# Pooled attention and a Gelu MLP on one core: the order of the first loads, w_in's halves, q's transposes of batch 1 and the last store

## The chip, the cores and the metric

The kernel runs on one core of a Trainium2 chip. The core has TensorE (PE), VectorE (DVE), ScalarE (ACT), GpSimd (POOL) and SyncE (SP), and 16 DMA engines which the queues of SP, ACT and POOL share. The metric is the device time of one execution in microseconds; lower is better.

## What is computed

```python
# q, k, v: (8 batches, 8 heads, 576 positions, 64) float32
k_p = k.reshape(B, H, Sp, 8, D).mean(axis=3)        # Sp = 72: means of 8 neighbours
v_p = v.reshape(B, H, Sp, 8, D).mean(axis=3)
attn = softmax(q @ k_p.T / sqrt(D))
x = (attn @ v_p) laid out as (4608 tokens, 512)
h = x @ w_in                                        # w_in: (512, 2048)
g = gelu_tanh(h)
out = g @ w_out                                     # w_out: (2048, 512), out: (4608, 512) float32
```

The matmuls run in bf16 with float32 sums.

## The kernel before

**Tiling.** Attention goes by batch, 8 of them with 576 columns each; its result is written transposed into `xT` (512 features as KO = 4 blocks of 128 partitions, 4608 columns). The MLP goes by groups of 512 columns (NG = 9). In each group phase 1 (`p1_mm`, L396) makes 16 tiles `fo` of h, each from 4 matmuls over `ko`, and `gelu` (L402) writes them to `gT`; phase 2 (`p2_mm`, L405) makes 4 row tiles of 128 rows of the output, 16 matmuls each, which `store` (L408) copies out of PSUM and sends off as 4 DMAs of 32 rows. The attention of batch g + 1 is woven into group g: pooling and transposes hang on tiles of phase 1 through `side` and `plan`, and scores, exponentials and products on matmul numbers of phase 2 through `todo`. The order on every engine is the order of the program text.

**The loads.** k and v come in as float32, q and the weights are turned to bf16 by the DMA. Before any computing the queues are given, in this order: k of batch 0 and a rest of v on SP and ACT (`load_k`, L74 to L77), v of batch 0 on SP and ACT (`load_v`, L90: 64 partitions each), and on GpSimd's queue q of batch 0 in two halves (L95), the identity matrix, w_in in two halves (L114), k of batch 1 (L74, L75, L77), q of batch 1 (L95) and w_out in four quarters (L121). w_in's halves are halves of its 2048 columns, each with all 4 blocks of rows: `w_in_b[0]` serves `fo` 0 to 7 and `w_in_b[1]` serves 8 to 15. v of batch 1 is issued on SP once VectorE has written one element of its tile (L485).

**Batch 0.** It is computed by itself ahead of group 0. VectorE pools k (L150), TensorE transposes k (L212) and q (L236), then come scores (L267), exponentials on ScalarE (L274), sums of exponentials (L349), logarithms and reciprocals (L354, L356), and VectorE's pooling of v (`v_steps`, L150 on `vt`, into `vz`), the products (L363) and the scaling into `xT` (L367). `spin` (L421) is a matmul of zeros that keeps TensorE busy. Group 0's first eight matmuls take `fo` 0 to 3 with `ko` 0 and 1, the next eight the same with `ko` 2 and 3.

**Batch 1, in group 0.** `plan` puts k's pooling at tile 0, `v_moves` (L183, a small DMA issued by ScalarE) at tile 7, the four transposes of q (`QG`) at tiles 12 to 15, with those of k at 13, and the pooling of half of v at 15. Attention starts in phase 2 at matmul number 6.

**The end.** The last row tile of the last group is made as two pieces of 384 and 128 columns (L617 to L626). Each is copied by VectorE and sent off as 4 DMAs of 32 partitions, two on ACT and two on SP:

```python
for n in range(4):
    b, col = divmod(N - 128 + n * 32, S)
    rows = out[b * S:(b + 1) * S].rearrange("(p t e) d -> e t p d", t=TP, e=2)
    (nc.sync if n % 2 else nc.scalar).dma_start(
        out=rows[col // CH, col % CH // 32][:, c0:c1], in_=osb[n * 32:(n + 1) * 32])
```

The 128 columns of `gT` that make a row tile stand as 4 blocks of 32, and rows that are neighbours within a block lie 18 output rows apart.

The softmax here doesn't subtract the row's maximum and nothing guards it: scores larger than these inputs give would overflow.

## Time and profile before

| what | us |
|---|---|
| median of 3 runs | 302.13 (302.08 to 303.34) |
| profiled execution | 303.02 |
| its span | 301.2 |
| TensorE busy, of the span | 292.1 |
| q, first half of batch 0: issue to landing | 8.2 |
| w_in, two halves: issue to landing | 14.6 and 19.4 |
| k of batch 1: issue to landing | 22.4 |
| last matmul ends | 297.4 |

The profile is one execution, taken by the hardware profiler. Its span is counted from the first instruction; all times below are from there. A line of the timeline gives start, length, engine, line, operation and tiles, and in brackets the idle time before it and what ended that. DMA issues have a line of their own with a q at the engine's name (SPq, ACTq); their length is that of issuing, not of the transfer. In the chain of waits each piece released the next.

### The profile page before, as it was taken

How to read it: one execution, taken by the hardware profiler on the slowest of the kernel's cores; microseconds unless marked ns; L12 is line 12 of the kernel's file. 1: busy time of each engine (PE TensorE's matmuls, PEld its weight loads, DVE VectorE, ACT ScalarE, POOL GpSimd, SP SyncE). 2: the span in 40 equal slices, each digit the busy share in tenths (PEclk: the TensorE clock that was granted, in tenths of full speed). 3: DMA queues.
4: the chain of work that ended last, by engine and by line, in shares of the span. 5: the costliest groups of instructions: out<-in, count | busy, mean ns of one | idle time of the engine just before them, and what ended most of it. 6: DMA issues, size and time to landing. Idle time of an engine off the chain costs nothing.

```text
span 301.2 us, 4348 instructions
## 1 busy us (share of the span) xinstructions
PE 292.1 (97%) x1498; PEld 151.4 (50%) x1527; DVE 149.6 (50%) x299; ACT 216.6 (72%) x408; POOL 37.6 (12%) x67
## 2 busy tenths in 40 slices
PE   8899999999999999999999999999999999999994
PEld 3465555554555455545554555455545555445443
DVE  3775577484577256815690659155924630110012
ACT  1596589879978898789877988798879887206500
POOL 7104001300600060005000410032000000000000
PEclk9999999999999999999999999999999999999998
DMA  7999986970798269935994399729961310121022
GB/s 223 263 242 268 252 175 127 255 185 12 169 265 174 48 153 248 187 72 120 247 202 89 90 254 208 106 51 252 236 119 36 74 37 0 37 70 36 0 72 70
DMA packets 39366, 43.11 MB, mean 143 GB/s; under 512 B 25584, under 2 KB 26224, under 8 KB 39216
## 3 DMA queue, kind: packets, MB, share of 16 engines
q0 software_dynamic: 8512, 24.39, 35.7%
q1 hardware_dynamic: 30080, 17.13, 25.0%
q10 hardware_dynamic: 752, 1.32, 1.3%
q8 instruction: 12, 0.20, 0.3%
q14 instruction: 10, 0.08, 0.1%
HBM read 36.70 MB, written 9.44 MB: 153 GB/s over the span
## 4 chain that ended last, share of the span: by engine, by line
PE 87%; DMA 7%; POOL 1%; DVE 1%; issue 1%; ACTq 0%; ACT 0%; DVEq 0%; POOLq 0%
PE PS L405 41%; PE PS L396 38%; DMA kt<-in_v_dram 7%; PE PS L322 4%; PE PS L311 2%; DVE kt L150 1%; PE PS L296 1%; PE PS L287 1%; PE PS L267 1%; POOL w_in_b L114 0%; POOL qb L95 0%; PE PS L236 0%; ACTq L183 0%; ACT gT L402 0%; POOL kt L74 0%
## 5 line engine op out<-in xcount | busy, mean ns | idle before, releaser
L405 PE MATMUL PS<-w_out_b,gT 128*128 128x512 bf16 (+2 forms) x575 | 138.0, 373 | 0.9 <-issue 0.2
L396 PE MATMUL PS<-xT,w_in_b 128*128 128x512 bf16 x565 | 125.9, 379 | 1.0 <-ACT gT L402 0.4
L402 ACT ACTIVATE gT<-PS 128x512 bf16<-128x512 f32 x144 | 79.2, 606 | 46.2 <-PE PS L396 46.2
L396 PEld LDWEIGHTS <-w_in_b 128*128 128x128 bf16 x576 | 65.0, 113 | 59.1 <-issue 0.7
L405 PEld LDWEIGHTS <-gT 128*128 128x128 bf16 x592 | 56.5, 97 | 52.5 <-issue 1.7
L340 DVE TENSOR_TENSOR xT<-PS,rc 64x288 bf16<-64x288 f32 x112 | 51.0, 455 | 20.5 <-ACT rc L332 17.8
L410 DVE COPY osb<-PS 128x512 f32<-128x512 f32 x35 | 24.2, 691 | 64.7 <-PE PS L405 61.4
L317 ACT ACTIVATE eT<-PS 64x576 bf16<-64x576 f32 x48 | 30.7, 640 | 0.6
L304 DVE COPY eT<-er 8x576 bf16<-8x576 bf16 x24 | 7.3, 302 | 39.9 <-ACT er L302 39.4
L329 ACT ACTIVATE ld<-PS 64x288 f32<-64x288 f32 x56 | 22.5, 402 | 5.6 <-PE PS L322 5.1
L332 ACT ACTIVATE rc<-ld 128x288 f32<-128x288 f32 x56 | 24.8, 443 | 1.8
L373 ACT ACT_TABLE_LOAD x17 | 21.8, 1283 | 3.6 <-issue 3.3
L150 DVE TENSOR_TENSOR kt<-kt 128x1280 f32<-128x1280 f32 (+5 forms) x18 | 18.9, 1048 | 10.0 <-DMA kt<-in_v_dram 6.0
L330 ACT ACTIVATE ld<-PS 64x288 f32<-64x288 f32 x56 | 22.5, 402 | 1.4
L322 PE MATMUL PS<-eT,vp 72*128 72x288 bf16 x96 | 19.7, 285 | 0.1
L150 DVE TENSOR_TENSOR vt<-vt 128x1024 f32<-128x1024 f32 (+3 forms) x18 | 17.1, 952 | 1.1 <-DMA vt<-in_v_dram 0.8
L502 POOL COPY gate<-eT 1x2 bf16<-1x2 bf16 x5 | 0.9, 177 | 125.6 <-DMA eT<-er 125.6
L322 PEld LDWEIGHTS <-vp 72*128 72x128 bf16 x96 | 9.5, 98 | 11.3
L421 PE MATMUL PS<-idle 128*128 128x512 bf16 x32 | 10.4, 466 | 1.6 <-DVE idle L139 1.2
L274 ACT ACTIVATE e<-PS 72x576 bf16<-72x576 f32 x16 | 9.9, 644 | 2.6 <-PE PS L267 2.4
L311 PE MATMUL PS<-qT,kx 128*128 128x288 bf16 x48 | 9.8, 286 | 0.0
L82 POOL DMA_DIRECT2D kt<-in_k_dram x12 | 7.5, 630 | 2.1 <-issue 2.1
(61 smaller groups left out, 115.0 us busy)
## 6 DMA issues: line engine op xcount, KB each, us to landing
out_dram<-osb SPq DMA_DIRECT2D x140, 64.0 KB
kt<-in_k_dram POOLq DMA_DIRECT2D x12, 512.0 KB, 6.5
vt<-in_v_dram POOLq DMA_DIRECT2D x12, 512.0 KB, 10.2
qb<-in_q_dram POOLq DMA_DIRECT2D x7, 576.0 KB, 14.7
w_in_b<-in_moe_w_in_dram POOLq DMA_DIRECT2D x2, 1024.0 KB, 17.0
w_out_b<-in_moe_w_out_dram POOLq DMA_DIRECT2D x4, 512.0 KB, 24.1
vt<-in_v_dram SPq DMA_DIRECT2D x3, 512.0 KB
kt<-in_k_dram POOLq DMA_DIRECT2D x1, 1024.0 KB, 22.4
```

What stands on the lines that cost most here:

```text
L150: nc.vector.tensor_tensor(out=o, in0=a, in1=b, op=ALU.add)
L317: nc.scalar.activation(out=eT[0:64, 2 * pr:2 * pr + 2, c, :], in_=PS[64 * c:64 * c + 64, 2:4, :CH], func=ACT.Exp, scale=1.0 / 64.0)
L322: nc.tensor.matmul(out=PS[:, bank + x, :CH], lhsT=window(vps[b % 2], 2 * pr + x), rhs=eT[:, 2 * pr + x, c, :], start=True, stop=True)
L329: nc.scalar.activation(out=ld[0:64], in_=PS[64:128, bank, :CH], func=ACT.Ln)
L330: nc.scalar.activation(out=ld[64:128], in_=PS[0:64, bank + 1, :CH], func=ACT.Ln)
L332: nc.scalar.activation(out=rc, in_=ld, func=ACT.Exp, scale=-1.0)
L340: nc.vector.tensor_tensor(out=xT[rows, pr, col:col + CH], in0=PS[rows, bank + x, :CH], in1=rc[rows], op=ALU.mult)
L373: nc.scalar.preload_act_table_set(name)
L396: nc.tensor.matmul(out=PS[:, h_bank(g, fo), :], lhsT=w, rhs=xT[:, ko, r0:r0 + GROUP], start=(ko == 0), stop=(ko == KO - 1))
L402: nc.scalar.activation(out=gTs[g][:, fo, :], in_=PS[:, h_bank(g, fo), :], func=ACT.Gelu_apprx_tanh)
L405: nc.tensor.matmul(out=PS[:, bank, c0:c1], lhsT=gTs[g][:, fo, r * 128:(r + 1) * 128], rhs=w_out_b[:, fo, c0:c1], start=(fo == 0), stop=(fo ...
L410: nc.vector.tensor_copy(out=osb, in_=PS[:, bank])
```

## The change

Four edits.

- **The loads.** `load_v(0)` stands behind `load_k(1)`, after a new GpSimd memset of one element of its tile, so that SP and ACT issue it when GpSimd has come that far in its own queue.
- **w_in.** The halves are halves of its rows: `w_in_b[0]` holds `ko` 0 and 1 for all 2048 columns, `w_in_b[1]` holds `ko` 2 and 3. `p1_mm` picks its operand accordingly.
- **q of batch 1.** Three of its four transposes and k's move one tile later in `plan`; the fourth goes into phase 2 at matmul number 2.
- **The last row tile.** VectorE copies its 128 columns of `gT`, four tiles at a time, into the idle `kts` tiles in another order (position in the block outermost, block innermost). The matmuls of the last row tile take these copies, so that the rows come out in an order in which 4 neighbouring partitions belong to 4 rows of `out` at a fixed distance, and each piece is one DMA of 128 partitions: ACT's for the 384 columns, SP's for the 128.

```diff
-    w_in_b = [consts.tile([128, KO, 1024], BF16, name=f"w_in_b{i}") for i in range(2)]
+    w_in_b = [consts.tile([128, KO // 2, DF], BF16, name=f"w_in_b{i}") for i in range(2)]
...
     load_k(0, [nc.sync, nc.scalar])
-    load_v(0, [nc.sync, nc.scalar])
     load_q(0, 0, 1)
     load_q(0, 1, 2)
     make_identity(nc, identb)
 
     def load_w_in(i):
-        nc.gpsimd.dma_start(out=w_in_b[i], in_=w_in_v[:, :, i * 1024:(i + 1) * 1024])
+        nc.gpsimd.dma_start(out=w_in_b[i], in_=w_in_v[:, 2 * i:2 * i + 2])
 
     load_w_in(0)
     load_w_in(1)
     load_k(1, [nc.gpsimd])
+
+    nc.gpsimd.memset(vts[0][:, 0, 0:1], 0.0)
+    load_v(0, [nc.sync, nc.scalar])
     load_q(1)
...
-        q, j = divmod(fo % 8, 4)
-        w = w_in_b[fo // 8][:, ko, q * 512 + j:(q + 1) * 512:4]
+        q, j = divmod(fo, 4)
+        w = w_in_b[ko // 2][:, ko % 2, q * 512 + j:(q + 1) * 512:4]
...
-                plan = {0: kk[:-1], 7: kk[-1:], 12: tq[:1], 13: tq[1:2] + tk, 14: tq[2:3], 15: tq[3:] + [lambda: v_half(1, 0)]}
+                plan = {0: kk[:-1], 7: kk[-1:], 13: tq[:1], 14: tq[1:2] + tk, 15: tq[2:3] + [lambda: v_half(1, 0)]}
...
+        if g + 1 == NG:
+
+            gLs = [kts[i // 2].rearrange("p r c -> p (r c)").bitcast(BF16)[:, i % 2 * 512:i % 2 * 512 + 512]
+                   .rearrange("p (f c) -> p f c", f=4) for i in range(4)]
+            for i, o in enumerate(gLs):
+                side[4 * i + 3].append(lambda i=i, o=o: nc.vector.tensor_copy(
+                    out=o.rearrange("p f (x t) -> p f t x", t=4),
+                    in_=gTs[g][:, 4 * i:4 * i + 4, 384:].rearrange("p f (t x) -> p f t x", t=4)))
...
             if g == 0:
+                at(2, trans_q, nb, *QG[3], 5, nc.vector)
                 at(18, v_half, 1, 1)
...
-            p2_mm(g, 3, fo, bank, c0, c1)
+            nc.tensor.matmul(out=PS[:, bank, c0:c1], lhsT=gLs[fo // 4][:, fo % 4], rhs=w_out_b[:, fo, c0:c1],
+                             start=(fo == 0), stop=(fo == FO - 1))
         osb = opool.tile([128, c1 - c0], F32, name="osb")
         nc.vector.tensor_copy(out=osb, in_=PS[:, bank, c0:c1])
-        for n in range(4):
-            b, col = divmod(N - 128 + n * 32, S)
-            rows = out[b * S:(b + 1) * S].rearrange("(p t e) d -> e t p d", t=TP, e=2)
-            (nc.sync if n % 2 else nc.scalar).dma_start(
-                out=rows[col // CH, col % CH // 32][:, c0:c1], in_=osb[n * 32:(n + 1) * 32])
+        b, col = divmod(N - 128, S)
+        t = col % CH // 32
+        rows = out[b * S:(b + 1) * S].rearrange("(p t e) d -> e p t d", t=TP, e=2)
+        (nc.sync if c0 else nc.scalar).dma_start(out=rows[col // CH, :, t:t + 4, c0:c1], in_=osb)
```

## The prediction

> **What bounds the kernel now.** I read the page first, then the chain of waits, the timeline of the first 45 us and of the last 8, the view of v's tile, and the trace's list of DMA packets (start, queue, size, duration).

> From the page, the engines' share of the span:

> ```profile
> PE 292.1 (97%) x1498; PEld 151.4 (50%) x1527; DVE 149.6 (50%) x299; ACT 216.6 (72%) x408; POOL 37.6 (12%) x67
> ```

> TensorE is the bound nearly everywhere, and its matmuls are not changed in number. What can move the time is what starts them, at the front, and what follows the last one. The chain of waits of the first 60 us (start, length, what) says what holds TensorE last at the front:

> ```profile
> 5.63 22.58 DMA kt<-in_v_dram
> ...
> 28.33 1.50 DVE kt L150
> ...
> 31.24 0.71 ACTq L183
> ...
> 32.64 1.02 PE PS L396 x4
> ```

> Batch 1's pooled rows land at 28.21, VectorE sums them until 31.2, ScalarE issues L183 and resumes Gelu at 31.99; TensorE, which had run without a gap from 21.72 to 32.25, waits 0.39 us. So this load hides whatever the front gains before it, beyond what the load itself gains. The timeline before that shows the other chain, that of v of batch 0:

> ```profile
> 1.84 22.92 SPq L90 DMA_DIRECT2D vt<-in_v_dram  x3
> 2.60 0.68 ACTq L90 DMA_DIRECT2D vt<-in_v_dram  x1
> 5.63 0.66 POOL L77 DMA_DIRECT2D kt<-in_v_dram  x1
> 9.52 0.68 PE L236 MATMUL PS<-identb,qb 128*128 128x128 bf16 x9 [0.54 <-DMA qb<-in_q_dram]
> 15.50 1.95 DVE L150 TENSOR_TENSOR vt<-vt 128x1024 f32<-128x1024 f32 x2
> 17.49 0.87 DVE L150 TENSOR_TENSOR vz<-vt 64x256 bf16<-64x256 f32 x2
> 18.25 0.65 PE L363 MATMUL PS<-e,vz 72*128 72x288 bf16 x4
> 21.72 10.53 PE L396 MATMUL PS<-xT,w_in_b 128*128 128x512 bf16 x47
> ```

> VectorE takes v up at 15.50 with no idle time before it; v's last packets ended at 13.7, so v has 1.8 us to spare. From there the path is tight: sums, vz, L363, first MLP matmul 6.2 us later. The end:

> ```profile
> 296.50 0.56 DVE L621 COPY osb<-PS 128x384 f32<-128x384 f32 x1 [1.91 <-DMA out_dram<-osb]
> 297.08 1.71 SPq L625 DMA_DIRECT2D out_dram<-osb  x4
> 297.09 1.80 ACTq L625 DMA_DIRECT2D out_dram<-osb  x4
> 297.39 0.29 DVE L621 COPY osb<-PS 128x128 f32<-128x128 f32 x1 [0.34 <-PE PS L405]
> ```

> Both queues issue one after another until 298.9; the last packet is at 299.84 and the span ends at 301.2.

> [...] from 28 to 38 us GpSimd's queue ran 419 packets (w_out's took 322 ns) and SP's 432 (96 ns): equal in number, not in bytes. [...] The trace shows the ramp (the spin's weight loads stand 0.43 us apart until 5.87, then 0.21)[...].

> **The change part by part.**

> *v of batch 0.* Both v loads now wait for a GpSimd memset, placed behind the issues of L77 and ahead of q of batch 1. L77's issue ends at 6.29; w_in's issues took 0.76 us each with 512 row pieces, and with 256 I put them at 0.63 (the other loads of 256 pieces took 0.63 to 0.65), so v is let go at about 6.1 instead of 1.84 and 2.60. Behind the wait on SP stand only batch 1's v loads, issued at 24.1; on ScalarE the table load, which moves from 3.31 to about 6.9 to 8.2, ahead of the first activation (10.01). On GpSimd the memset costs 0.1 us ahead of loads that are not urgent.

> When does v land? Issue to first packet on free DMA engines: 297.08 to 298.13, 1.05 us. Under load it is more: batch 1's v, issued at 24.10, had its first packet at 27.78; L183, at 31.24, at 35.53. In these stretches, less 1.05, each engine served 13 and 17 other data packets, so some 14 are queued ahead of a newcomer. At 7.2 these are about 9 of q's (191 ns) and 5 of w_in's. w_in's pieces double: 8 KB read and 4 KB written, as w_out's, which take 322 ns. So 9 x 0.191 + 5 x 0.322 = 3.3 us, first packet at 10.5. Then each engine has 16 packets of v on SP's queue and 16 on ScalarE's, turn about with w_in: 96 + 84 + 322 = 502 ns, 16 times, 8.0 us. (In the kernel before v shared with q: 96 + 84 + 191 = 371 ns, 5.9 us; trace: 6.9 to 12.6 on SP's queue.) Mean end 18.5, slowest engine and semaphore 0.5 more: v lands at about 19.0, 3.5 us after VectorE wanted it. With 8 packets ahead it is 17.2, with 17 it is 20.0.

> From VectorE's start the old path holds, 15.50 to 21.60 (weight load of the first MLP matmul), less 0.2 us since the reciprocals (L356) are ready: 19.0 + 5.9 = 24.9, 3.3 us late. TensorE then needs no wait at 32.25, as batch 1's k is long there: 3.3 - 0.39 = 2.9 us lost.

> *q earlier.* Without v, q's 128th packet ends near 7.7 instead of 8.0 and its slowest engine near 8.0 instead of 8.69; L236 can start at 8.98, behind the k transposes, instead of 9.52. This 0.54 us would carry through scores and exponentials, but ends at VectorE's wait for v: worth nothing, unless v is in time.

> *w_in by rows.* 1024 packets x 173 ns become 512 x 322: (177.2 - 164.9)/16 = 0.77 us less on each engine ahead of batch 1's k, which then lands at 27.4. That would be worth 0.77 us if this chain came last; behind v's it hides. The second half is needed eight matmuls (1.7 us) into the MLP, at about 26.6; the bytes ahead of it put it near 22.5.

> *q of batch 1 a tile later.* The same 36 transposes. VectorE starts the copies of L248 and L219 0.86 us later (one fo tile of four 0.215 us matmuls), and has one copy less (0.42) ahead of v_half: 0.44 us later against TensorE, where the first L287 had 0.3 us to spare (vp ready at 40.45, taken at 40.77). I take a loss of 0.1 us; bounds 0 and 0.4.

> *The last row tile.* Four VectorE copies of 128x512 bf16 (nearest row: L248's 128x512 at 0.42; I bound one at 1 us for its stride) fall into VectorE's idle time from 269.7 to 287 and are needed at 293.7: free. The last store becomes one DMA on SP, issued at 297.70 when the copy ends, instead of the second of a queued pair at 298.4: first packet at 298.75, and the 16 packets per engine of both DMAs (8 x 105 + 8 x 28 ns, from 298.1) end at 299.2 instead of 299.8. Gain 0.6 us; bounds 0.3 (a 128-row issue of 0.6 us) and 0.8.

> Sum: 2.9 + 0.1 - 0.6 = +2.4 us. Against the profiled execution, 303.02 (span 301.2 and 1.8 around it), that is 305.4; this one stood 0.9 over the median of 302.13, so the median becomes 304.5.

> **Rivals.**

> *v nearly in time.* Only 8 packets are ahead: v at 17.2, VectorE 1.7 late, MLP 1.5 late, 1.1 lost after the 0.39: 1.1 + 0.1 - 0.6 gives 302.7. For it: the mix ahead of v is not the one of my two samples. Against: both samples lie above it.

> *v in time (not slower).* v lands by 15.0, because its two queues get more than a packet's turn against w_in, or w_in's packets stay short. Then only batch 1's k counts: TensorE resumes at 32.64 - 0.77 = 31.87, its own work being ready at 32.25 - 0.54 = 31.71. Gain 0.77 and 0.6 of the tail: 300.7. It decides from v at 15.0. The equal packet counts from 28 to 38 us speak against it.

> *The clock falls too.* TensorE, out of work at about 18.0, waits for v until 21.4: 3.4 us[...].

> That v is not let go later after all can be excluded: both loads wait on GpSimd in the built program.

> **How the numbers follow.** Main case 0.50 (own range 303.5 to 305.5, from v at 18.0 to 20.0), nearly in time 0.20, in time 0.15, clock 0.15. About 0.5% (1.5 us) is what a measurement tells from no change: slower means above 303.6, faster below 300.6. The main case is above 303.6 for 0.46 of its 0.50, the clock wholly: slower 0.61. In time straddles 300.6: faster 0.08. The rest, 0.31, is within. Low end 301.3 leaves out most of the in-time case, high end 306.0 most of the clock's.

> **What would show it.** Right: L150 on vt starts near 19 with idle time charged to in_v; L396 starts near 25; no idle time before L396 at fo 8; batch 1's k lands a little earlier than before; w_in's packets are 4096 B at about 320 ns, and v's run one for one with them. Wrong: L150 on vt with no wait near 15, or L396 near 21; the last packets later than 299.5 against the last copy's old place; weight loads 0.43 us apart after 21 (the clock).

## The result

The changed kernel takes 310.40 us (median of 6 runs, 309.14 to 310.91) against 302.19 for the kernel before: a ratio of 1.026, interval 1.024 to 1.029. That is 8.2 us slower, above the range of the prediction. Later comparisons on the chip put the kernel before at 302.4 to 302.6; each ratio below stands against the runs of its own comparison.

The page gives TensorE's busy share and its granted clock (the share of full speed that it was allowed), each in tenths, in 40 slices; a 9 is 90% or more. The kernel before, in slices of 7.5 us:

```profile
PE   8899999999999999999999999999999999999994
...
PEclk9999999999999999999999999999999999999998
```

The changed kernel, in slices of 7.7 us:

```profile
PE   8849999999999999999999999999999999999995
...
PEclk9985999999999999999999999999999999999999
```

The third and fourth slices (15 to 31 us) are where the time went: a 4 in TensorE's busy share, and then an 8 and a 5 in the clock. From the first matmul of group 1 on nothing more is lost: that one came 7.6 us later than before (63.03 against 55.39), and the last matmul ended 7.6 us later (304.99 against 297.35).

The timeline of the changed kernel at the same places as before:

```profile
6.34 24.21 SPq L90 DMA_DIRECT2D vt<-in_v_dram  x3
6.34 0.70 ACTq L90 DMA_DIRECT2D vt<-in_v_dram  x1
...
16.96 0.60 PE L423 MATMUL PS<-idle 128*128 128x512 bf16 x2
...
19.28 1.95 DVE L152 TENSOR_TENSOR vt<-vt 128x1024 f32<-128x1024 f32 x2 [4.66 <-DMA vt<-in_v_dram]
21.27 0.87 DVE L152 TENSOR_TENSOR vz<-vt 64x256 bf16<-64x256 f32 x2
21.74 1.14 PE L365 MATMUL PS<-e,vz 72*128 72x288 bf16 x4 [4.18 <-DVE vz L152]
...
27.48 2.76 PE L398 MATMUL PS<-xT,w_in_b 128*128 128x512 bf16 x6
...
30.47 11.34 PE L398 MATMUL PS<-xT,w_in_b 128*128 128x512 bf16 x49 [0.22 <-issue]
```

v is let go at 6.34, VectorE waits 4.66 us for it, and TensorE, whose last matmul of zeros ended at 17.56, waits 4.18 us for vz. Then the same work takes longer: the four products L365 last 1.14 us instead of 0.65, and from the first product to the first MLP matmul it is 5.7 us instead of 3.5. The view of two-microsecond stretches says why (stretch and its length, then busy time and count of PE, weight loads, DVE, ACT and POOL, then granted clock, DMA share, GB/s):

```profile
18.00:20.00 2.00, 0.00 (x0) 0.00 (x0) 0.72 (x1) 0.79 (x2) 0.00 (x0) 1.00 1.11 229
20.00:22.00 2.00, 0.26 (x2) 0.17 (x3) 1.90 (x4) 0.00 (x0) 0.00 (x0) 0.86 1.04 281
22.00:24.00 2.00, 2.00 (x10) 1.29 (x9) 0.90 (x2) 0.16 (x1) 0.54 (x2) 0.50 0.98 406
...
30.00:32.00 2.00, 1.78 (x6) 0.77 (x6) 1.84 (x3) 0.00 (x0) 0.00 (x0) 0.58 1.03 207
```

The trace's clock records give it to the hundredth: half clock from 21.43 to 31.67, 10.24 us. In the profile of the kernel before the clock is full from 5.91 to 299.45. The chain of waits now runs through v, no longer through batch 1's k (start, length, what):

```profile
6.21 0.12 POOL vt L119
...
6.34 12.86 DMA vt<-in_v_dram
...
19.28 1.24 DVE vt L152
...
21.74 1.14 PE PS L365 x4
```

So the reading to be tested is this: v is late by its place in the queues, and the clock falls while TensorE waits for it. The rivals are three: w_in by rows costs by itself; the slow clock is only a passenger, because something else sets the pace; v's lateness has nothing to do with w_in's packets.

### The profile page after: what moved, and what is told of

The parts are those of the page before. It is cut to its first block, busy times and chain, and to the rows that moved or that the text cites. A ratio compares the mean times of both kernels' runs of the same rounds, so it can differ in the third digit from the quotient of the medians.

```text
span 308.7 us, 4347 instructions
## 1 busy us (share of the span) xinstructions
PE 296.2 (96%) x1498; PEld 152.5 (49%) x1527; DVE 152.5 (49%) x303; ACT 217.1 (70%) x408; POOL 37.5 (12%) x68
## 4 chain that ended last, share of the span: by engine, by line
PE 91%; DMA 4%; POOL 2%; issue 1%; DVE 1%; DVEq 0%; POOLq 0%
PE PS L398 41%; PE PS L407 39%; DMA vt<-in_v_dram 4%; PE PS L324 4%; PE PS L313 2%; PE PS L365 1%; PE PS L631 1%; PE PS L289 1%; PE PS L298 1%; PE PS L269 1%; DVE vt L152 1%; POOL w_in_b L113 0%; POOL qb L95 0%; PE PS L238 0%; PE PS L423 0%
## 5 line engine op out<-in xcount | busy, mean ns | idle before, releaser
L407 PE MATMUL PS<-w_out_b,gT 128*128 128x512 bf16 x543 | 134.6, 379 | 0.8 <-issue 0.2
L398 PE MATMUL PS<-xT,w_in_b 128*128 128x512 bf16 x565 | 127.5, 383 | 0.7 <-issue 0.2
L407 PEld LDWEIGHTS <-gT 128*128 128x128 bf16 x560 | 53.9, 97 | 51.2 <-issue 2.0
L331 ACT ACTIVATE ld<-PS 64x288 f32<-64x288 f32 x56 | 22.5, 403 | 5.6 <-PE PS L324 5.2
L332 ACT ACTIVATE ld<-PS 64x288 f32<-64x288 f32 x56 | 22.5, 402 | 1.4
L544 DVE COPY kt<-gT 128x512 bf16<-128x512 bf16 x4 | 3.0, 744 | 11.6 <-ACT gT L404 11.6
## 6 DMA issues: line engine op xcount, KB each, us to landing
vt<-in_v_dram POOLq DMA_DIRECT2D x12, 512.0 KB, 10.5
kt<-in_k_dram POOLq DMA_DIRECT2D x1, 1024.0 KB, 22.5
```

The source lines that it names most:

```text
L331: nc.scalar.activation(out=ld[0:64], in_=PS[64:128, bank, :CH], func=ACT.Ln)
L332: nc.scalar.activation(out=ld[64:128], in_=PS[0:64, bank + 1, :CH], func=ACT.Ln)
L398: nc.tensor.matmul(out=PS[:, h_bank(g, fo), :], lhsT=w, rhs=xT[:, ko, r0:r0 + GROUP], start=(ko == 0), stop=(ko == KO - 1))
L407: nc.tensor.matmul(out=PS[:, bank, c0:c1], lhsT=gTs[g][:, fo, r * 128:(r + 1) * 128], rhs=w_out_b[:, fo, c0:c1], start=(fo == 0), stop=(fo ...
```

## The experiments

**v back at the start, the other three edits kept.**

```diff
     load_k(0, [nc.sync, nc.scalar])
+    load_v(0, [nc.sync, nc.scalar])
...
-    nc.gpsimd.memset(vts[0][:, 0, 0:1], 0.0)
-    load_v(0, [nc.sync, nc.scalar])
```

> The changed kernel, with v of batch 0 let go at the start again (the other three edits kept). Theory A (v lands late behind w_in's packets, and TensorE's clock falls while it waits): VectorE takes v up at about 15.5 without waiting, no matmul runs at half clock after 21 us, batch 1's k lands about 0.8 us earlier than before so that the 0.39 us wait at fo 8 is gone, q's later turn costs 0.4: 301.8 to 302.3 us. Rival B (w_in by rows is what costs, its second half coming late or its larger packets crowding others out): it stays within 2 us of the changed kernel, 308 or more.

Measured: 302.94 us, ratio 1.0016 (1.0001 to 1.003). That is 0.6 us above the range expected: VectorE, at 15.48, has still waited 0.70 us for v. All but 0.5 us of the loss is gone with this one edit. **w_in by rows alone**, on the kernel before, says the same of the rival:

```diff
-        nc.gpsimd.dma_start(out=w_in_b[i], in_=w_in_v[:, :, i * 1024:(i + 1) * 1024])
+        nc.gpsimd.dma_start(out=w_in_b[i], in_=w_in_v[:, 2 * i:2 * i + 2])
```

> The kernel before, with w_in in halves of its rows and nothing else. Theory A: each DMA engine saves 0.77 us ahead of batch 1's k, the wait of 0.39 us at fo 8 goes, v still lands in time: 301.6 to 301.9 us. Rival B (w_in by rows costs): 304 or more.

Measured: 302.96 us, ratio 1.0012 (0.9996 to 1.0028): no difference that can be told, and not the gain of half a microsecond that was expected. In its profile VectorE now waits for v, 0.60 us up to 15.53. v's last packet ends at 14.84 instead of 13.29, beside w_in packets of twice the bytes.

**The clock kept up.** The changed kernel with 20 more matmuls of zeros in the time of the wait:

```diff
-    spin(2, 4)
+    spin(22, 4)
     av0(0, 0, 4)
```

> The changed kernel, with 22 instead of 2 matmuls of zeros ahead of the first product with v (20 more, 4.3 us at full clock, in the time in which TensorE waits for v). Theory A: the clock does not fall, the first product still starts near 21.7, the first MLP matmul near 25.3 instead of 27.25, and the ten microseconds at half clock are gone: 305.0 to 306.0 us. Rival C (the clock is only a passenger, since ScalarE's and VectorE's chain behind v sets the pace of the front): 309 or more.

Measured: 306.81 us, ratio 1.0143 (1.0128 to 1.0158), 3.6 us under the changed kernel. The matmuls of its timeline:

```profile
17.27 4.91 PE L423 MATMUL PS<-idle 128*128 128x512 bf16 x22
22.02 0.66 PE L365 MATMUL PS<-e,vz 72*128 72x288 bf16 x4
...
25.50 1.68 PE L398 MATMUL PS<-xT,w_in_b 128*128 128x512 bf16 x7
```

No idle time is shown before the products, they take 0.66 us again, and the MLP starts 2.0 us earlier although the products start 0.3 us later. The next phase starts 4.1 us earlier (first matmul with w_out at 40.37 instead of 44.43). The clock is no passenger. It is not the whole loss either: 4.4 us remain, and the time is 0.8 us above the range expected.

**v held back, w_in by columns.** The kernel before with the first edit only: the same place in the queues, but w_in in packets of 2048 B.

```diff
-    load_v(0, [nc.sync, nc.scalar])
...
     load_k(1, [nc.gpsimd])
+    nc.gpsimd.memset(vts[0][:, 0, 0:1], 0.0)
+    load_v(0, [nc.sync, nc.scalar])
```

> The kernel before, with v of batch 0 let go behind k of batch 1 and nothing else: w_in keeps its halves by columns and its 2048 B packets of 173 ns. Theory A with packets taken in turn: a turn of three queues is 96 + 84 + 173 = 353 ns instead of 502, so v's 16 turns take 5.6 us instead of 8.0 and v lands near 16.0, against 19.2 in the changed kernel; TensorE's gap is under 2 us and the clock stays: 302.0 to 303.0 us. Rival D (the lateness comes from letting v go at 6.3 us by itself, w_in's packets play no part): v lands at 19 again and the clock falls: 308 or more.

Measured: 303.69 us, ratio 1.0060 (1.0033 to 1.0087), 0.7 us above the range expected; and the clock did not stay in every run, since four of the nine have a mean granted clock of 0.986 to 0.992. Its timeline:

```profile
6.41 19.41 SPq L90 DMA_DIRECT2D vt<-in_v_dram  x3
...
16.86 1.95 DVE L152 TENSOR_TENSOR vt<-vt 128x1024 f32<-128x1024 f32 x2 [1.57 <-DMA vt<-in_v_dram]
...
19.32 0.66 PE L365 MATMUL PS<-e,vz 72*128 72x288 bf16 x4 [1.08 <-DVE vz L152]
```

v is let go at nearly the same moment and its first packet starts at 10.3, as in the changed kernel (10.4), but its last packet on SP's queue starts at 15.9 instead of 18.2: 5.6 us from first to last instead of 7.8. 16 turns of 353 ns are 5.6 us; 16 turns of 502 ns are 8.0.

**v on one queue.** The turns again, from the other side:

```diff
-    load_v(0, [nc.sync, nc.scalar])
+    load_v(0, [nc.sync])
```

> The changed kernel, with both halves of v of batch 0 on SP's queue instead of one on SP's and one on ScalarE's. Packets in turn: a turn is now 96 + 322 = 418 ns and each engine has 32 of v's packets on one queue, 13.4 us instead of 8.0, so v's packets run from about 10.4 to 24 and VectorE takes v up near 24.5 instead of 19.3: about 5 us later still, 314 to 317 us. If the DMA engines shared by bytes, or by DMA, one queue or two would matter little: v near 19 to 20 and 309 to 312.

Measured: 316.58 us (two runs), ratio 1.047 (1.045 to 1.049). v's first packet starts at 10.27 and its last at 23.68: 13.4 us, as counted. VectorE's and TensorE's lines, from its timeline:

```profile
24.89 1.95 DVE L152 TENSOR_TENSOR vt<-vt 128x1024 f32<-128x1024 f32 x2 [9.96 <-DMA vt<-in_v_dram]
```

```profile
27.36 1.14 PE L365 MATMUL PS<-e,vz 72*128 72x288 bf16 x4 [9.48 <-DVE vz L152]
```

The same bytes of v, the same neighbours, one queue instead of two: v comes 5.6 us later than in the changed kernel (24.89 against 19.28). For these loads sharing by packets in turn is shown; sharing by bytes, which would have brought v near 19 to 20, is out.

**Half the matmuls of zeros.** How long must a gap be to cost the clock? The changed kernel with 10 more matmuls of zeros:

```diff
-    spin(2, 4)
+    spin(12, 4)
     av0(0, 0, 4)
```

> The changed kernel, with 12 instead of 2 matmuls of zeros ahead of the first product with v: the gap on TensorE shrinks from 4.2 us to about 2.2 (v held back alone had 1.1 us and kept its clock). If the clock is lost to the length of an unbroken gap and 2.2 us is still short enough: as with 22 of them, 306.5 to 307.1. If 2.2 us is enough to lose it: 309 or more.

Measured: 309.56 us, ratio 1.0236 (1.0222 to 1.0251), but not as one value: one run took 306.73 us at full clock throughout (its profile shows a gap of 1.87 us and no change of clock ahead of the kernel's end), and five took 308.17 to 309.77 with a mean granted clock of 0.986 to 0.992. The first products of the run at full clock:

```profile
21.96 0.66 PE L365 MATMUL PS<-e,vz 72*128 72x288 bf16 x4 [1.87 <-DVE vz L152]
```

A gap of this length sometimes costs the clock (five runs) and sometimes not (one). A second profile of the same kernel caught the other case:

> The changed kernel with 12 matmuls of zeros once more, to see in a profile what five of its six runs did: a gap of about 1.9 us on TensorE before the first product with v, and the granted clock at 0.5 for some 7 us from 21 or 22 on; 309.5 us. If the profile shows full clock throughout at 309.5, those runs lost their time elsewhere.

Measured: 309.55 us (two runs). The matmuls in its timeline, and below them its stretches:

```profile
22.05 0.66 PE L365 MATMUL PS<-e,vz 72*128 72x288 bf16 x4 [1.98 <-DVE vz L152]
22.55 0.65 PE L351 MATMUL PS<-e,ones 72*128 72x288 bf16 x4
23.04 1.71 PE L365 MATMUL PS<-e,vz 72*128 72x288 bf16 x8
```

```profile
22.00:24.00 2.00, 1.95 (x14) 1.44 (x15) 1.38 (x3) 0.33 (x1) 0.41 (x1) 0.90 0.99 410
24.00:26.00 2.00, 2.00 (x9) 0.94 (x7) 1.31 (x2) 1.92 (x4) 2.00 (x2) 0.50 1.08 231
...
30.00:32.00 2.00, 2.00 (x9) 0.94 (x8) 1.97 (x3) 0.61 (x2) 0.00 (x0) 0.89 1.07 215
```

The gap is over at 22.05, and the four products and four sums (L351) after it still run at full clock; the clock falls at 23.60, 1.5 us into the work, and comes back at 30.43. So a gap of 1.98 us was enough here, and its price falls on what comes after it. What the traces show of this is in the last section.

**The gap of the kernel with v held back alone, filled.**

```diff
-    spin(2, 4)
+    spin(10, 4)
     av0(0, 0, 4)
```

> The kernel before with v held back alone, and 8 more matmuls of zeros ahead of the first product with v (1.7 us, about the whole of the gap). Without them 4 of 9 runs had a mean clock of 0.992 or less and took 304.7 to 306.6 us, the others about 303.6. If those four lost the clock in the 1.1 to 1.6 us gap: all or nearly all runs at 0.997 or more and 303.3 to 304.0. If they lost it elsewhere: as many slow ones as without.

Measured: 304.07 us, ratio 1.0058 (1.0041 to 1.0075). All four runs (303.73 to 304.24) have a mean clock of 0.999 or more, but the median did not get better. Eight matmuls more delay the products by 0.12 us (19.44 instead of 19.32), which is a part of it; the rest is not explained. With four runs against nine this agrees with a loss in a gap of 1.1 us; it does not prove it.

**The other two edits, each alone on the kernel before.**

> The kernel before, with the new last row tile alone (VectorE's copies, one store per piece). From the changed kernel's trace, where 3.73 us lie between the last matmul's end and the span's end instead of 3.89: 0.1 to 0.2 us less than before, 302.1 to 302.3. The prediction's 0.6 us would give 301.6 to 301.8.

> The kernel before, with batch 1's q turned a tile later alone. Theory A: phase 2 of group 0 grows by 0.6 us (18.6 instead of 18.0, of which 0.2 are the four transposes that moved into it), and phase 1 gives 0.2 to 0.6 back: from no change to 0.4 us slower, 302.1 to 302.7. Rival: 1 us or more lost, were the changed kernel's growth in phase 2 due to this edit and not given back.

Measured: the new last row tile 302.39 us, ratio 0.9996 (0.9988 to 1.0004); q's later turn 302.70 us, ratio 1.0008 (0.9994 to 1.0022). Neither can be told from no change. Of the tail the profiles say a little more: 3.70 us lie between the end of the last matmul and that of the span, against 3.89. In phase 2 of group 0 with q's later turn the first two products with v of batch 1 take 0.61 us instead of 0.41, because a weight load waits 0.3 us for VectorE's later pooling. In the profiles phase 2 is 0.6 us longer than before and phase 1 is 0.8 us shorter; 0.4 us of that is the wait at `fo` 8, which this execution does not have.

**A candidate.** Batch 1's k needs to land early, and the second half of w_in, by columns, is not needed before `fo` 8. The kernel before with these two issues exchanged, and the new last row tile:

```diff
     load_w_in(0)
-    load_w_in(1)
     load_k(1, [nc.gpsimd])
+    load_w_in(1)
```

> A candidate: the kernel before, with k of batch 1 issued ahead of the second half (by columns) of w_in, and the new last row tile. 1024 packets of w_in's two halves took 177 us of engine time, so half of them is 5.5 us: k lands near 23 instead of 28.2, VectorE's and ScalarE's chain at fo 8 is over before TensorE needs it and the 0.39 us wait goes; w_in's second half lands near 25.5 and is needed at fo 8, at about 29. With the tail's 0.16: 301.5 to 301.8. If w_in's second half comes too late instead: a new wait at fo 8 and 302.5 or more.

Measured: 302.04 us, ratio 0.9976 (0.9967 to 0.9986): 0.5 us faster than before (0.4 to 1.0 by the interval), 0.2 us short of the range expected; the tail alone gave nothing that can be told. Its timeline:

```profile
21.77 10.52 PE L396 MATMUL PS<-xT,w_in_b 128*128 128x512 bf16 x48
...
24.70 2.28 DVE L150 TENSOR_TENSOR kt<-kt 128x1280 f32<-128x1280 f32 x2
...
28.07 0.73 ACTq L183 DMA_DIRECT2D vp<-kp  x1
```

VectorE sums k at 24.70 with no wait for it, ScalarE's L183 no longer stands behind it, and TensorE runs through `fo` 8 without its gap. It has the lowest ratio of all kernels here.

## Why the prediction was wrong

**v of batch 0, when it lands: right.** Predicted: let go at 6.1, first packet at 10.5, each engine's last packet at 18.5 in the mean, VectorE at 19.0. Measured: 6.34, 10.4, the last packet of all ends at 18.55, 19.28. A little luck is in this. The packet times quoted in the prediction stand 0.24 us late against the timeline, so the free delay from issue to first packet was 0.8 us and not 1.05; that cancels against v being let go 0.24 us later than forecast. The turn of one packet per queue is shown by three kernels (5.6, 7.8 and 13.4 us from v's first packet to its last; VectorE takes v up at 16.86, 19.28 and 24.89), and by a count: while v moved in the changed kernel, from 10.41 to 18.3, SP's queue started 256 packets, ScalarE's 254 and GpSimd's 262. The rivals with v in time and nearly in time are out.

**The clock: this step failed.** It was the last rival, with a chance of 0.15 and a price that was the author's estimate, since no trace had shown how long the clock stays down. Both were too low. All six runs of the changed kernel have a mean clock of 0.981 to 0.989, and with a gap of 1.9 to 2.0 us 7 of 8 runs lost the clock already. And the price was 3.6 us in the medians (310.40 against 306.81; 3.8 if each is taken over the kernel before of its own comparison): the clock stayed down for 10.24 us. The prediction named the view that would show this (weight loads 0.43 us apart after 21); it should have given this case the main place: the wait of 3.4 us that it forecast on TensorE itself is longer than the 1.9 to 2.0 us which cost the clock in those runs.

**The size of v's lateness: this term was short by more than a microsecond.** 2.9 us were predicted for it and 2.4 in sum; with the clock kept, 4.4 us remain, and 306.81 is above the range even without the clock's part. The working measured from 15.50, where VectorE took v up in the profiled execution of before. But in that execution q came late (0.54 us of waiting before L236), and it stood 0.9 us over the median. In the profile with the new tail alone, whose front is that of the kernel before, L236 starts at 8.80 without waiting and VectorE takes v up 0.7 us earlier. Below it is the same step in the kernel with the 22 matmuls of zeros:

```profile
14.79 1.95 DVE L150 TENSOR_TENSOR vt<-vt 128x1024 f32<-128x1024 f32 x2
...
19.20 1.95 DVE L152 TENSOR_TENSOR vt<-vt 128x1024 f32<-128x1024 f32 x2 [4.28 <-DMA vt<-in_v_dram]
```

From there v is 4.4 us late. Less the gap at `fo` 8 that is gone (0.34 us in the profile with the tail alone), and with the 0.3 us by which the zeros delay the products, this makes, but for some hundredths, the 4.35 us by which the two spans differ (304.64 and 300.29). The prediction took v's lateness from a long execution, in which VectorE was itself late, and then lowered the whole sum by 0.9 us to reach the median. These are single profiles, and the early loads move by some tenths: with q's later turn alone VectorE takes v up at 15.44 without waiting for q. So this part is uncertain by about half a microsecond.

**q earlier: right, and worth nothing,** as said: L238 starts at 8.66 and the gain ends at VectorE's wait. **w_in by rows: right in its packets** (4096 B, some 325 ns each), **and right that its 0.77 us hide behind v.** The rival with v in time counted them as a gain. With v let go at the start no such gain shows (302.94 and 302.96 us), and in both of these profiles VectorE waits for v, whose neighbour's packets are now longer.

**Batch 1's q:** no change that can be told, which agrees with the bounds. **The tail: mis-sized,** 0.2 us in the profiles instead of 0.6. The one DMA of 128 partitions takes 0.65 us to issue, and its first packet came 1.3 us after the issue began; I had used the delay of a 32-partition store.

```profile
304.14 0.56 DVE L634 COPY osb<-PS 128x384 f32<-128x384 f32 x1 [1.91 <-DMA out_dram<-osb]
304.73 0.64 ACTq L638 DMA_DIRECT2D out_dram<-osb  x1
305.03 0.29 DVE L634 COPY osb<-PS 128x128 f32<-128x128 f32 x1 [0.34 <-PE PS L631]
305.35 0.65 SPq L638 DMA_DIRECT2D out_dram<-osb  x1
```

VectorE's four copies cost 0.74 us each in its idle time and delay nothing. This is the timeline of the changed kernel; of the lines of before, four issues in a row on each queue have become one.

The prediction also held fixed what the time has beyond the span, 1.8 us. It moves with the tail: it is 1.73 to 1.85 us in all 136 runs of kernels with the old tail for which the record has the span, and 2.06 to 2.25 us in all 69 with the new one. These 0.3 us are more than the 0.2 us won between the last matmul and the end of the span; what fills them no trace shows.

## What to carry to other kernels

A transfer that was let go later lost twice here: it waited 4 us among what was already on its way before its first packet moved, and from then on it got a turn per packet and not per byte: 5.6 us from first packet to last beside packets of 173 ns, 7.8 us beside packets of 322 ns. When a new wait falls on TensorE, price the clock as well as the wait: fill the gap with matmuls of zeros in one run, and the difference (3.6 us here) is the clock's share. Measure lateness from an execution that stands for the median, not from one that happened to wait somewhere else. Judge an edit of the last store by the time and not by the span alone.
